# One-go logits, an early first list and waiting remainders in a convolution with mixture of experts

## The chip, the cores and the metric

The kernel runs on one core of one Trainium2 chip. Its time is the device time of one execution in microseconds (us), as a median over runs. PE is the matrix engine (TensorE), DVE the vector engine, ACT the scalar engine, POOL the general engine that issues the scatters here, and SP the engine that issues nearly all other transfers (DMAs). Each engine runs its own instructions strictly in program order and waits, where it must, for the others.

## The reference

A causal convolution over each sequence, whose seven weights per token and head are a softmax, is followed by a mixture of experts in which each token goes to one group of experts and to one expert in it:

```python
w = np.exp(weight_gen - max); w = w / (sum + 1e-09)          # (8, 2880, 8 heads, 7)
out = einsum('bshk,bskhg->bshg', w, x_unfolded)              # 192 = 8 heads x 24
g_idx = argmax(x @ w_group)                                  # 4 groups, weight g_w from their softmax
e_idx = argmax(xg @ w_expert[g])                             # 4 experts of the group, weight e_w
h = np.maximum(xg[mask_e] @ w1[g, e], 0.0)                   # 192 -> 1024
out[tok_idx] = (g_w * e_w)[:, None] * (h @ w2[g, e])         # 1024 -> 192
```

There are 8 × 2880 = 23040 tokens of 192 numbers and 16 experts in all, everything in 32-bit floats.

## The kernel before

The tokens are cut into 15 groups of 1536 (128 partitions × 12 rows), a group into two chunks of 6 rows per partition. For one group after the other `front()` yields the work of the convolution and of the routing in small steps, and a planner, which keeps a clock of its own for each engine (`clk`, `run`), writes the steps into one program order per engine. `Until(t)` holds a step back until the planner's DVE clock is at t, `NEXT` until one more unit is written, `Chunk(o, n)` until n chunks of the group are done. `move(qs, q, most)` takes up to `most` steps of a side task. After the planner nothing is reordered: what stands behind a waiting instruction on its engine waits too.

**Convolution.** `conv(g, o)` makes seven products per chunk on DVE (L280, tile `pr`, three buffers). In the first ten chunks (`TURNED = 10`, groups 0 to 4) PE adds each product and turns it over in the same step, by nine matmuls with the identity (L319, into three pieces of PSUM named `ph`, `py` and `tpx`). Such a set of nine is called a unit here. After a chunk's seventh unit ACT copies the three pieces out (L325, tiles `hl` and `xlo`). In later chunks DVE adds (L298) instead. `softmax(g)` (L255 to L268) makes a group's seven weights, on DVE with one exp on ACT.

**Routing.** `route(g, o)` turns the sums of a group back into rows (L390 on PE, called a back here, and L400 on ACT, into `xrow`), makes the logits (L365), turns them (L417), copies them to `ls` (L420), finds group and expert by `first_max` on DVE, counts tokens per expert with matmuls, and gets from that the position of each row (`posi`, L483). Twelve scatters on POOL (L513) then put the rows of the group into `rows` in memory, sorted by expert. At the end of each round of groups (`ROUNDS`; the first, `FIRST = 2`, is groups 0 and 1) `table` writes the work list `tab` (L590, L595).

**Visits.** A visit takes one block of rows of one expert through both matrices. The first round has ten plain visits of 128 rows, 0 to 9: SP reads the list (L745, L754), loads the rows (L746, tile `xb`), w1 (L757, two loads into `wa`) and w2 (L766, `wc`); PE turns the rows (L833) and does the two products, called gemm1 (L865) and gemm2 (L892). The later rounds have main visits of 256 rows (L841 turns their rows), with w1 split in two parts of lower precision: ACT casts (L779, L782), DVE subtracts (L797). The last 64 rows of w1 have their remainders ready in memory, as `w1lo`. The units of conversion and routing of later groups lie between the matmuls of the visits.

**Remainders.** `halves()` makes `w1lo` once, in eight pieces of two experts: loads on SP (L603, tile `raw`), cast on ACT (L612), subtract on DVE (L614), two stores on SP (L616). Before, it has two buffers, and a piece's loads are asked one piece ahead. The pieces are spread over the convolution of the first groups: one step in every fourth product, and the rest when the first main round comes up.

**Fillers.** `warm()` (L214) writes matmuls of no use into a free corner of PSUM where the planner thinks that PE would wait before the visits begin.

`blocks()` starts a round's visits: it asks the loads of the first visits in the order w1, w2, rows, one visit after the other.

Of the kernel before, what the change touches and what calls it, by code (L numbers as in the profile page):

```python
# [8 lines left out]
F32 = mybir.dt.float32  # L9
# [23 lines left out]
def conv_moe_kernel(ctx: ExitStack, tc: tile.TileContext, x, wgen, w_group, w_expert, w1, w2, out):  # L33
# [156 lines left out]
    state = {"slots": False, "open": False, "unit": 0, "starve": False, "ph": 0, "junk": None}  # L190
# [80 lines left out]
    sums, evac, spread = [], [], []  # L271
# [79 lines left out]
    def route(g, o):  # L351
# [17 lines left out]
        xTs = []  # L369
        txT = 0.0  # L370
        for s2 in range(0, SG, 2):
            n, i = s2 // SC, s2 % SC // 2
            if o.chunks <= n:
                yield Chunk(o, n + 1)
            row = xrow[n][:, s2 % SC:s2 % SC + 2, :]
            turned = n in o.turned
            if turned:
                txT = max(txT, evac[-1])
            elif i == 0:
                rem = rt.tile([P, SC, HP], F32, name="rem")  # L380
                nc.scalar.copy(out=rem, in_=xrow[n][:, :, P:D])
                txT = run("act", 0.4, clk["dve"])
                yield NEXT
            warm(txT)
            ttp = run("pe", 0.35, txT)
            tp = ps_t.tile([P, 3, P], F32, name="tp")
            if turned:
                xT = o.turned[n][i]
                for c in range(3):
                    nc.tensor.transpose(out=tp[:, c, :], in_=xT[:, c, :], identity=ident)  # L390
            else:
# [3 lines left out]
            if len(xTs) == 2:  # L395
                run("pe", 0.5, txT)
                logits(s2 - 4, xTs)
                xTs = []
            if turned:
                nc.scalar.copy(out=row[:, :, 0:D], in_=tp.rearrange("p c q -> p (c q)").rearrange("p (s d) -> p s d", s=2))  # L400
                run("act", 0.48, ttp)
            else:
# [3 lines left out]
            xTs.append((xT, turned))  # L406
            yield NEXT
        run("pe", 0.5, txT)
        logits(SG - 4, xTs)
# [3 lines left out]
        yield NEXT  # L413
# [6 lines left out]
        nc.scalar.copy(out=ls, in_=lps.rearrange("p q (j l) -> p (q j) l", l=LW)[:, :, 0:NL])  # L420
        for c, row in enumerate(xrow):
            nc.vector.tensor_copy(out=row.bitcast(I32)[:, :, D + 1:D + 2], in_=ii[:, s0 + c * SC:s0 + (c + 1) * SC].unsqueeze(2))
        yield 0.3
        yield Until(run("act", 0.4, clk["pe"]) + LATE[1])
# [35 lines left out]
        yield Until(tt + LATE[0])  # L460
# [25 lines left out]
        if g < MAIN:  # L486
            yield from finish_all(spread)
        if 0 < g < MAIN or g + 1 == ENDS[-1]:
            for c in rest:
                if g >= MAIN:  # L490
                    yield c
            if g + 1 in ENDS:
                yield from table(round_of(g))
            return
# [104 lines left out]
    def halves():  # L599
        def fetch(e):  # L600
            raw = new_raw[0]()
            for h in range(2):
                nc.sync.dma_start(out=raw[h * HP:(h + 1) * HP, :], in_=w1v[e + h, P:D, :])  # L603
            return raw

        hi = new_raw[2]()[:, 0:F].bitcast(F32R)
        nxt = fetch(0)
        for e in range(0, NE, 2):
            raw = nxt
            if e + 2 < NE:  # L610
                nxt = fetch(e + 2)
            nc.scalar.copy(out=hi, in_=raw)  # L612
            yield Until(run("act", 0.95))
            nc.vector.tensor_tensor(out=raw.bitcast(F32R), in0=raw, in1=hi.bitcast(F32), op=ALU.subtract)  # L614
            for h in range(2):
                nc.sync.dma_start(out=w1lo[e + h], in_=raw[h * HP:(h + 1) * HP, :])  # L616
            yield 1.13

# [15 lines left out]
    def front():  # L634
# [4 lines left out]
        slow = [[halves(), None]]  # L639
        yield from softmax(0)  # L640
        for g in range(ENDS[-1]):
            o = grp[g]
            routes.append([route(g, o), None])
            for n, c in enumerate(conv(g, o)):
# [6 lines left out]
                if n % 4 == 2:  # L651
                    for q in list(slow):
                        yield from move(slow, q, 1)
                for q in side[:1]:
                    yield from move(side, q, 3)
# [4 lines left out]
            if g + 1 == MAIN:  # L660
                yield from finish_all(slow)
# [67 lines left out]
    def load(n, part):  # L729
# [12 lines left out]
        if part == 0:  # L742
# [9 lines left out]
            return  # L752
        if o.ev is None:
            o.ev = nc.sync.value_load(tab[q:q + 1, 1:2], min_val=0, max_val=NE - 1)  # L754
# [179 lines left out]
    def blocks(n0, n1, paced):  # L934
# [59 lines left out]
        for n in range(n0, min(n0 + 2, n1)):  # L994
# [109 lines left out]
```

## Time and profile before

| | us |
|---|---|
| time before, median of 3 runs (1261.15 to 1261.85) | 1261.33 |
| time of the profiled execution | 1262.81 |
| its span | 1261.1 |
| opening, to visit 0's first matmul | 143.76 |
| ten plain visits, to the first turning of main rows | 102.12 |
| passage, to the first main gemm1 | 13.66 |
| main visits and tail | 1001.56 |

PE is busy for 1200.4 us of the span (95%), DVE for 921.7 (73%), ACT for 662.9 (53%) and POOL for 421.4 (33%). The granted clock of PE is 0.984 of the full speed on average. An engine's busy time includes the fillers. The span is what the profiler records between the first and the last instruction, and the time of the execution is a little longer.

### The profile page before, as it was taken

The page shows a single profiled execution, that of the slowest core. Times are in us where ns is not written, and L with a number is a line of the kernel's source. Part 1 is how long each engine was busy: PE and PEld are TensorE (multiplying, and loading weights), DVE is VectorE, ACT ScalarE, POOL GpSimd, SP SyncE. Part 2 cuts the span into 40 slices and gives each one's busy share as a digit, 9 for nine tenths or more (in the row PEclk, how much of TensorE's full clock was granted, in tenths as well). Part 3 has the DMA queues.
Part 4 walks back from the last instruction along what each step waited for, and adds up shares of the span by engine and source line. Part 5 has one row for each costly group of instructions (what it writes and reads, how often), then busy time and mean ns, then how long its engine had stood idle before and what let it go on. Part 6 is the DMA issues. An engine that isn't in the chain of part 4 may idle for free.

```text
span 1261.1 us, 26794 instructions
## 1 busy us (share of the span) xinstructions
PE 1200.4 (95%) x9559; PEld 1170.2 (93%) x9559; DVE 921.7 (73%) x1582; ACT 662.9 (53%) x1242; POOL 421.4 (33%) x412
## 2 busy tenths in 40 slices
PE   5998599899999999999999999999999999999995
PEld 5987599889999999999999999999999999999995
DVE  8974568788989999898899889961227677777500
ACT  1222133355555556555655565555556677767532
POOL 3043144143435243443524343453153311221111
PEclk9999799989999999999999999999999999999998
DMA  7447677988788879796979797778677877777792
GB/s 211 137 124 214 178 234 208 296 243 268 222 280 237 272 219 283 213 303 195 288 209 302 220 281 205 227 219 240 188 221 238 257 233 222 222 229 211 209 265 54
DMA packets 181678, 286.10 MB, mean 227 GB/s; under 512 B 16084, under 2 KB 141775, under 8 KB 181280
## 3 DMA queue, kind: packets, MB, share of 16 engines
q1 hardware_dynamic: 162304, 245.09, 66.6%
q0 software_dynamic: 19232, 39.22, 9.5%
q8 instruction: 77, 1.26, 0.4%
q14 instruction: 65, 0.53, 0.1%
HBM read 240.89 MB, written 44.33 MB: 226 GB/s over the span
## 4 chain that ended last, share of the span: by engine, by line
PE 62%; issue 19%; POOL 4%; DMA 3%; SPq 1%; POOLq 1%; DVE 1%; ACT 1%; ACTq 0%
PE py L892 27%; PE ph L865 26%; POOL out L909 3%; PE pl L365 2%; DMA raw<-in_moe_w 2%; PE tpx L841 1%; PE tpx L842 1%; PE tp L393 1%; PE ph L319 1%; PE py L319 1%; PE tpx L319 1%; DMA raw<-w1lo 1%; DMA rows<-xrow,posi 1%; PE tp L394 1%; POOLq L566 1%
## 5 line engine op out<-in xcount | busy, mean ns | idle before, releaser
L865 PE MATMUL ph<-xh,wa 128*128 128x256 f32 x2064 | 459.1, 299 | 0.0
L892 PE MATMUL py<-wc,hh 128*128 128x192 f32 x2240 | 417.6, 327 | 7.4 <-ACT xb L901 7.3
L909 POOL DMA_INDIRECT out<-xb x190 | 206.0, 1084 | 626.2 <-ACT xb L901 412.2
L892 PEld LDWEIGHTS py<-wc,hh 128*128 128x128 f32 x2240 | 359.6, 190 | 7.8 <-ACT xb L901 7.8
L865 PE MATMUL ph<-xlo,wa 128*128 128x256 f32 x1376 | 358.8, 282 | 0.0
L865 PEld LDWEIGHTS ph<-xh,wa 128*128 128x128 f32 x2064 | 350.1, 190 | 7.4 <-issue 5.9
L871 ACT ACTIVATE hh<-ph 128x512 f32<-128x512 f32 (+1 forms) x316 | 173.4, 549 | 314.8 <-PE ph L865 314.8
L280 DVE TENSOR_TENSOR pr<-xin,wt 128x1152 f32<-128x1152 f32 x190 | 253.8, 1352 | 18.2 <-PE tpx L319 18.1
L865 PEld LDWEIGHTS ph<-xlo,wa 128*128 128x128 f32 x1376 | 261.9, 190 | 0.0
L513 POOL DMA_INDIRECT rows<-xrow,posi x180 | 196.3, 1091 | 181.1 <-DVE posi L483 56.5
L797 DVE TENSOR_TENSOR wa<-raw,wa 128x1024 fp32r<-128x1024 f32 x86 | 105.0, 1221 | 83.6 <-ACT wa L779 81.8
L298 DVE TENSOR_TENSOR xrow<-xrow,pr 128x1152 f32<-128x1152 f32 x120 | 162.4, 1353 | 0.6
L894 PE MATMUL py<-wc,hh 128*128 128x384 f32 x400 | 122.6, 362 | 0.8 <-DVE xb L907 0.8
L797 DVE SCALAR_TENSOR_TENSOR hl<-ph,hh 128x512 fp32r<-128x512 f32 x100 | 69.1, 691 | 67.8 <-ACT hh L876 67.5
L895 PE MATMUL py<-wc,hl 128*128 128x192 f32 x400 | 100.6, 251 | 0.0
L779 ACT CAST wa<-raw 128x1024 fp32r<-128x1024 f32 x86 | 90.3, 1050 | 8.9 <-DMA raw<-in_moe_w 8.9
L782 ACT CAST wa<-raw 128x1024 fp32r<-128x1024 f32 x86 | 89.5, 1040 | 0.3 <-DMA raw<-w1lo 0.3
L901 ACT ACTIVATE xb<-py,xb 128x192 f32<-128x192 f32 x190 | 71.7, 421 | 27.5 <-PE py L892 21.9
L865 PE MATMUL ph<-xd,wa 96*128 96x128 f32 x576 | 77.3, 277 | 0.5 <-ACT xd L835 0.5
L894 PEld LDWEIGHTS py<-wc,hh 128*128 128x128 f32 x400 | 76.0, 190 | 1.2 <-DVE xb L907 1.2
L895 PEld LDWEIGHTS py<-wc,hl 128*128 128x128 f32 x400 | 77.1, 193 | 0.0
L797 DVE TENSOR_TENSOR xlo<-tpx,xh 128x512 fp32r<-128x512 f32 x86 | 59.2, 688 | 23.2 <-ACT xh L846 23.0
(165 smaller groups left out, 1326.4 us busy)
## 6 DMA issues: line engine op xcount, KB each, us to landing
wc<-in_moe_w SPq DMA_DIRECT2D x79, 768.0 KB, 7.6
raw<-in_moe_w SPq DMA_DIRECT2D x86, 512.0 KB, 4.2
raw<-in_moe_w SPq DMA_DIRECT2D x102, 256.0 KB, 4.3
xin<-in_x SPq DMA_DIRECT2D x26, 864.0 KB, 8.2
raw<-w1lo SPq DMA_DIRECT2D x86, 256.0 KB, 5.2
raw<-in_moe_w SPq DMA_DIRECT2D x25, 768.0 KB, 4.9
xb<-rows SPq DMA_DIRECT2D x86, 194.0 KB, 4.2
wa<-in_moe_w SPq DMA_DIRECT2D x36, 384.0 KB, 4.1
```

The source lines that it names most:

```text
L280: nc.vector.tensor_tensor(out=dst, in0=o.xin[:, c0 + k:c0 + k + SC, :].rearrange("p s (h g) -> p s h g", g=HG), in1=w4[:, c0:c0 + SC, :, k ...
L298: nc.vector.tensor_tensor(out=acc, in0=acc, in1=prs[k - 2], op=ALU.add)
L513: written_once(nc.gpsimd.indirect_dma_start(out=rows[:, :], out_offset=bass.IndirectOffsetOnAxis(ap=idx, axis=0), in_=src, in_offset=None, ...
L779: nc.scalar.copy(out=o.wa[:, 0, :], in_=o.raw[0])
L782: nc.scalar.copy(out=o.wa[:, 2, :], in_=o.raw[1])
L797: f(*a, **k)
L865: nc.tensor.matmul(ph[:, v, :], lhsT=w[:, f0:f0 + P], rhs=rhs, start=i == 0, stop=i == len(terms) - 1)
L871: nc.scalar.activation(out=hh, in_=ph, func=AF.Relu)
L892: nc.tensor.matmul(b.py[t][:, 0:D], lhsT=hh[:, v, c], rhs=wc[0][:, f, :], start=f == 0, stop=f == NFT - 1)
L894: nc.tensor.matmul(b.py[t], lhsT=hh[:, v, c], rhs=wc[f // 4][:, f % 4].rearrange("p l d -> p (l d)"), start=f == 0, stop=False)
L895: nc.tensor.matmul(b.py[t][:, 0:D], lhsT=hl[:, v, c], rhs=wc[f // 4][:, f % 4, 0, :], start=False, stop=f == NFT - 1)
L909: ins = nc.gpsimd.indirect_dma_start(out=out[:, :], out_offset=bass.IndirectOffsetOnAxis(ap=b.x.bitcast(I32)[:, t, D + 1:D + 2], axis=0), ...
```

## The change

All edits are in the planner and in the order of steps; the arithmetic stays.

- `route`: for groups with turned chunks the first chunk's three backs are written while the second chunk is convolved; after the second chunk come all 48 logits matmuls at once, one back, the turn of the logits, the copy to `ls`, and then the second chunk's other two backs. Other groups go the old way, in `forward()`.
- In groups 0 and 1 the planner's wait for `ls` and for the counts is 0.3 instead of `LATE`.
- `state["urgent"]` is set while group 2 (`FIRST`) is convolved and the first list isn't made; then the next group's softmax and the remainders stand still.
- `halves()` starts in group 1 and asks four pieces at once, into four buffers; subtracts come from group 2 on, after the first list; what is left is written before the first main weights.
- The scatters that are still to come are finished in one go before a list of an early round, and in the last groups' routing only every third is a step.
- `blocks()` asks the weights of the first three visits, then their three row loads.

```diff
-    sums, evac, spread = [], [], []
+    sums, evac, spread, slow = [], [], [], []
...
+        def back(n, i):
+            warm(evac[-1])
+            ttp = run("pe", 0.35, evac[-1])
+            tp = ps_t.tile([P, 3, P], F32, name="tp")
+            for c in range(3):
+                nc.tensor.transpose(out=tp[:, c, :], in_=o.turned[n][i][:, c, :], identity=ident)
+            nc.scalar.copy(out=xrow[n][:, 2 * i:2 * i + 2, 0:D], in_=tp.rearrange("p c q -> p (c q)").rearrange("p (s d) -> p s d", s=2))
+            run("act", 0.48, ttp)
...
+        turned = 2 * g < TURNED
+        if turned:
+            for i in range(NP):
+                back(0, i)
+                yield NEXT
+            yield Chunk(o, 2)
+            warm(evac[-1])
+            run("pe", 1.2, evac[-1])
+            flat = [(t, True) for n in range(2) for t in o.turned[n]]
+            for q in range(SG // 4):
+                logits(4 * q, flat[2 * q:2 * q + 2])
+        else:
+            yield from forward()
         lts = rt.tile([P, 3, P], F32, name="xT", bufs=2)
         nc.scalar.copy(out=lts, in_=lt)
         tlt = run("act", 0.48, clk["pe"])
-        yield NEXT
+        if turned:
+            back(1, 0)
+        else:
+            yield NEXT
...
+        tls = run("act", 0.4, clk["pe"])
+        if turned:
+            for i in range(1, NP):
+                back(1, i)
...
-        yield Until(run("act", 0.4, clk["pe"]) + LATE[1])
+        yield Until(tls + (0.3 if g < FIRST else LATE[1]))
...
-        yield Until(tt + LATE[0])
+        yield Until(tt + (0.3 if g < FIRST else LATE[0]))
...
         if g < MAIN:
-            yield from finish_all(spread)
+            while spread:
+                for c in spread.pop(0)[0]:
+                    pass
         if 0 < g < MAIN or g + 1 == ENDS[-1]:
-            for c in rest:
-                if g >= MAIN:
+            for i, c in enumerate(rest):
+                if g >= MAIN and i % 3 == 2:
                     yield c
             if g + 1 in ENDS:
                 yield from table(round_of(g))
+            state["urgent"] = False
             return
...
     def halves():
         def fetch(e):
-            raw = new_raw[0]()
+            raw = new_raw[e // 2 % 2]()
             for h in range(2):
                 nc.sync.dma_start(out=raw[h * HP:(h + 1) * HP, :], in_=w1v[e + h, P:D, :])
-            return raw
+            return raw, clk["dve"]
 
         hi = new_raw[2]()[:, 0:F].bitcast(F32R)
-        nxt = fetch(0)
+        got = [fetch(2 * e) for e in range(4)]
+        yield Until(clk["dve"] + 10.0)
         for e in range(0, NE, 2):
-            raw = nxt
-            if e + 2 < NE:
-                nxt = fetch(e + 2)
+            raw, t = got.pop(0)
+            yield Until(t + 18.0)
             nc.scalar.copy(out=hi, in_=raw)
...
             yield 1.13
+            if e and e + 6 < NE:
+                got.append(fetch(e + 6))
...
+            state["urgent"] = g == FIRST
             for n, c in enumerate(conv(g, o)):
...
-                if n % 4 == 2:
+                if g == FIRST - 1 and n == 4:
+                    slow.append([halves(), None])
+                    yield from move(slow, slow[0], 1)
+                if g >= FIRST and n % 2 == 0 and not state["urgent"]:
                     for q in list(slow):
-                        yield from move(slow, q, 1)
-                for q in side[:1]:
-                    yield from move(side, q, 3)
+                        yield from move(slow, q, 2)
+                if not state["urgent"]:
+                    for q in side[:1]:
+                        yield from move(side, q, 3)
...
-            if g + 1 == MAIN:
-                yield from finish_all(slow)
...
+        if not plain(n):
+            while slow:
+                assert step() is not False
...
-            ask(n, 0)
         if n0 + 2 < n1 and plain(n0 + 2):
             ask_w(n0 + 2)
-        ask_x(n0 + 2)
+            ask(n0 + 2, 3)
+        for n in range(n0, min(n0 + 3, n1)):
+            ask(n, 0)
+        if n0 + 2 < n1 and not plain(n0 + 2) and (whole(n0 + 2) or whole(n0 + 1)):
+            ask(n0 + 2, 3)
```

SP, behind visit 1's weights, before: the third visit's row load (`xb_160`), its w2, the last remainder's loads (L603) and four stores (L616), and group 4's weights (L238).

```order
L746 DMA xb_160<-rows 128x194
L766 ISA
L766 DMA wc<-in_moe_w 128x8x192
L603 DMA raw_170<-in_moe_w 64x1024 x2
L616 DMA w1lo<-raw_171 64x1024 x2
L616 DMA w1lo<-raw_170 64x1024 x2
L238 DMA wt<-in_weight_gen 128x672
```

The same place on SP in the changed program, where the row load is L770, the remainders' loads L623 and their stores L636:

```order
L770 DMA xb_160<-rows 128x194
L232 DMA xin<-in_x 128x1728
L636 DMA w1lo<-raw_171 64x1024 x2
L636 DMA w1lo<-raw_173 64x1024 x2
L623 DMA raw_171<-in_moe_w 64x1024 x2
L636 DMA w1lo<-raw_170 64x1024 x2
L623 DMA raw_173<-in_moe_w 64x1024 x2
L636 DMA w1lo<-raw_172 64x1024 x2
L623 DMA raw_170<-in_moe_w 64x1024 x2
L238 DMA wt<-in_weight_gen 128x672
```

The loads of the first four pieces (171, 173, 170, 172) have moved far ahead of this place, ahead of the first read of a list; the loads of three later pieces stand here instead, each behind the store that frees its buffer.

DVE, from the end of the first list (`done`) to the first maximum of group 2's routing, before:

```order
L561 SCALAR_TENSOR_TENSOR done<-tk,done 128x16
L280 TENSOR_TENSOR pr<-xin,wt 128x1152 x2
L422 COPY xrow<-ii 128x6 x2
L614 TENSOR_TENSOR raw_171<-raw_171,raw_174 128x1024
L614 TENSOR_TENSOR raw_170<-raw_170,raw_174 128x1024
L280 TENSOR_TENSOR pr<-xin,wt 128x1152
L333 TENSOR_REDUCE mxg<-ls 128x12
```

The same engine in the changed program, from the end of the first list (L581) on; L634 is the remainders' subtract, L255 to L268 is the softmax of group 3:

```order
L581 SCALAR_TENSOR_TENSOR done<-tk,done 128x16
L280 TENSOR_TENSOR pr<-xin,wt 128x1152
L255 TENSOR_REDUCE m<-wt 128x96
L257 TENSOR_TENSOR wt<-wt,m 128x672
L280 TENSOR_TENSOR pr<-xin,wt 128x1152 x2
L262 TENSOR_REDUCE z<-wt 128x96
L264 TENSOR_SCALAR z<-z 128x96
L266 RECIPROCAL z<-z 128x96
L634 TENSOR_TENSOR raw_171<-raw_171,raw_174 128x1024
L268 TENSOR_TENSOR wt<-wt,z 128x672
L280 TENSOR_TENSOR pr<-xin,wt 128x1152 x3
L634 TENSOR_TENSOR raw_173<-raw_173,raw_174 128x1024
```

Two products of chunk 5 were left when the list was done, ten are left now, and the subtracts have moved from the far side of the list to this one.

PE, the end of chunk 5's routing, before: backs (L390) and logits (L365) in turn, the logits' turn (L417), 60 fillers and chunk 6's first unit (L319).

```order
L390 MATMUL tp<-ident,xlo 128x128 x3
L365 MATMUL pl<-hl,wr 32x128 x8
L390 MATMUL tp<-ident,xlo 128x128 x3
L365 MATMUL pl<-xlo,wr 32x128 x8
L214 MATMUL py_1273<-ident 128x128 x2
L417 MATMUL pl<-ident,xT 128x128 x3
L214 MATMUL py_1273<-ident 128x128 x60
L319 MATMUL ph_1715<-ident,pr 128x128 x3
```

The same place on PE in the changed program, where a back is L374, the logits' turn L430, and L860 and L892 are visit 0's turn and gemm1:

```order
L214 MATMUL py_1398<-ident 128x128 x11
L365 MATMUL pl<-hl,wr 32x128 x16
L365 MATMUL pl<-xlo,wr 32x128 x8
L374 MATMUL tp<-ident,hl 128x128 x3
L430 MATMUL pl<-ident,xT 128x128 x3
L374 MATMUL tp<-ident,xlo 128x128 x6
L860 MATMUL tp<-ident,xb_158 96x128 x2
L892 MATMUL ph_1584<-xd_167,wa 128x128 x4
```

Visit 0's matmuls now stand directly behind chunk 5's routing, and chunk 6's first unit behind them.

SP, behind the weights of a main visit shortly before the first main gemm1, before: an input load (L232) stands between w1 of one visit and the rows of another.

```order
L762 DMA raw_172<-w1lo 64x1024
L232 DMA xin<-in_x 128x1728
L745 TENSOR_LOAD tab_1943
L745 ISA x2
L746 ISA
L746 DMA xb_160<-rows 128x388
```

The same place in the changed program:

```order
L789 DMA raw_172<-w1lo 64x1024
L769 TENSOR_LOAD tab_1908
L769 ISA x2
L770 ISA
L770 DMA xb_160<-rows 128x388
```

The input load has moved behind the w1 loads of three more main visits.

## Rows read from the trace of the kernel before

**Rows 1.** Stretches: length, engines' busy us (count), PEclk, DMA share, GB/s.
```profile
0.00:143.76 143.76, 107.81 (x993) 98.87 (x994) 104.66 (x200) 31.54 (x60) 35.08 (x50) 0.94 0.62 175
143.76:245.88 102.12, 100.69 (x883) 95.99 (x882) 82.54 (x167) 37.26 (x93) 36.63 (x32) 1.00 0.76 233
245.88:259.54 13.66, 6.33 (x35) 6.14 (x33) 5.64 (x7) 3.97 (x8) 0.97 (x1) 0.67 0.91 239
259.54:1261.10 1001.56, 985.61 (x7654) 969.22 (x7652) 728.83 (x1211) 590.13 (x1081) 348.74 (x329) 0.99 0.79 233
```

**Rows 2.** Waits in 0 to 262 us: total us, times, longest us.
```profile
PE ph L319 <- DVE pr L280: 30.9, 5, 15.0
DVE raw L614 <- ACT raw L612: 27.5, 2, 16.4
```

**Rows 3.** The chain in 105 to 146 us: start us, length us, what.
```profile
110.25 6.74 DMA rows<-xrow,posi
...
117.14 0.36 SPq L746
...
124.89 1.34 SPq L603
126.27 10.51 DMA raw<-in_moe_w
...
139.10 1.36 DVE pr L280
...
140.51 0.90 PE ph L319 x3
```

**Rows 4.** Three short or typical stretches, columns as in rows 1.
```profile
130.00:140.00 10.00, 0.00 (x0) 0.00 (x0) 2.04 (x2) 1.04 (x1) 0.00 (x0) 0.50 0.68 176
250.00:255.00 5.00, 0.00 (x0) 0.00 (x0) 0.74 (x1) 1.82 (x4) 0.00 (x0) 0.55 1.00 240
300.00:600.00 300.00, 300.00 (x2338) 293.31 (x2338) 271.65 (x456) 174.19 (x324) 121.21 (x106) 1.00 0.81 247
```

**Rows 5.** DVE in order of time: start, length, instruction, count, [idle before <-releaser].
```profile
79.18 1.36 DVE L280 TENSOR_TENSOR pr<-xin,wt 128x1152 f32<-128x1152 f32 x1 [6.56 <-PE tpx L319]
...
94.76 0.17 DVE L483 SCALAR_TENSOR_TENSOR posi<-pos 128x12 int32<-128x12 f32 x1
...
105.89 0.15 DVE L595 TENSOR_SCALAR tab<-ri 128x1 int32<-128x1 f32 x1
...
106.47 2.62 DVE L280 TENSOR_TENSOR pr<-xin,wt 128x1152 f32<-128x1152 f32 x2
```

**Rows 6.** DVE groups in 13.29 to 109.1 us: count, busy us, mean ns.
```profile
L280 DVE TENSOR_TENSOR pr<-xin,wt 128x1152 f32<-128x1152 f32 x42 | 55.0, 1352 | 6.9 <-PE tpx L319 6.9
L614 DVE TENSOR_TENSOR raw<-raw,raw 128x1024 fp32r<-128x1024 f32 x6 | 7.3, 1220 | 0.0
...
L255 DVE TENSOR_REDUCE m<-wt 128x96 f32<-128x672 f32 x3 | 2.5, 848 | 0.0
```

**Rows 7.** PE at chunk 5's end and visit 9's, as rows 5.
```profile
113.23 1.42 PE L214 MATMUL py<-ident 128*128 128x128 f32 x11 [0.29 <-ACT xlo L325]
...
115.55 0.55 PE L390 MATMUL tp<-ident,xlo 128*128 128x128 f32 x3 [0.57 <-ACT xrow L400]
...
117.14 0.65 PE L365 MATMUL pl<-xlo,wr 128*32 128x128 f32 x16
...
118.77 6.71 PE L214 MATMUL py<-ident 128*128 128x128 f32 x60
...
255.36 1.65 PE L892 MATMUL py<-wc,hh 128*128 128x192 f32 x4 [7.33 <-ACT xb L901]
```

**Rows 8.** POOL, first scatter of group 1, columns as in rows 5.
```profile
95.71 1.33 POOL L513 DMA_INDIRECT rows<-xrow,posi  x1 [11.38 <-issue]
```

**Rows 9.** The chain in 222 to 262 us, columns as in rows 3.
```profile
244.38 8.70 DMA raw<-in_moe_w
```

**Rows 10.** The page's DMA issues: count, KB each, median us to landing.
```profile
xb<-rows SPq DMA_DIRECT2D x86, 194.0 KB, 4.2
```

More of the change, by code (lines that the diff above doesn't have):

```diff
@@ L189, in conv_moe_kernel @@
     grp = {}
-    state = {"slots": False, "open": False, "unit": 0, "starve": False, "ph": 0, "junk": None}
+    state = {"slots": False, "open": False, "unit": 0, "starve": False, "ph": 0, "junk": None, "urgent": False}
     def ph_tile(k, shape):
@@ L367, in logits, with forward @@
                         start=u == 0, stop=u == 1, tile_position=(0, j * LW))
[L369 to L382, printed above, removed]
-                yield NEXT
-            warm(txT)
-            ttp = run("pe", 0.35, txT)
-            tp = ps_t.tile([P, 3, P], F32, name="tp")
[L387 to L391, printed above, removed]
+        def back(n, i):
+            warm(evac[-1])
+            ttp = run("pe", 0.35, evac[-1])
+            tp = ps_t.tile([P, 3, P], F32, name="tp")
+            for c in range(3):
+                nc.tensor.transpose(out=tp[:, c, :], in_=o.turned[n][i][:, c, :], identity=ident)
+            nc.scalar.copy(out=xrow[n][:, 2 * i:2 * i + 2, 0:D], in_=tp.rearrange("p c q -> p (c q)").rearrange("p (s d) -> p s d", s=2))
+            run("act", 0.48, ttp)
+        def forward():
+            xTs = []
+            for s2 in range(0, SG, 2):
+                n, i = s2 // SC, s2 % SC // 2
+                if o.chunks <= n:
+                    yield Chunk(o, n + 1)
+                row = xrow[n][:, s2 % SC:s2 % SC + 2, :]
+                if i == 0:
+                    rem = rt.tile([P, SC, HP], F32, name="rem")
+                    nc.scalar.copy(out=rem, in_=xrow[n][:, :, P:D])
+                    txT = run("act", 0.4, clk["dve"])
+                    yield NEXT
+                ttp = run("pe", 0.35, txT)
+                tp = ps_t.tile([P, 3, P], F32, name="tp")
                 for u in range(2):
@@ L394, in route @@
                 nc.tensor.transpose(out=tp[:, 2, :], in_=rem[:, s2 % SC:s2 % SC + 2, :].rearrange("p s d -> p (s d)"), identity=ident)
[L395 to L402, printed above, removed]
+                if len(xTs) == 2:
+                    run("pe", 0.5, txT)
+                    logits(s2 - 4, xTs)
+                    xTs = []
                 xT = rt.tile([P, 3, P], F32, name="xT", bufs=2)
@@ L405, in route @@
                 txT = run("act", 0.48, ttp)
[L406 to L409, printed above, removed]
+                xTs.append((xT, False))
+                yield NEXT
+            run("pe", 0.5, txT)
+            logits(SG - 4, xTs)
+        turned = 2 * g < TURNED
+        if turned:
+            for i in range(NP):
+                back(0, i)
+                yield NEXT
+            yield Chunk(o, 2)
[6 more added lines that the diff above has]
+            yield from forward()
         lts = rt.tile([P, 3, P], F32, name="xT", bufs=2)
@@ L412, in route @@
         tlt = run("act", 0.48, clk["pe"])
-        yield NEXT
+        if turned:
+            back(1, 0)
+        else:
+            yield NEXT
         warm(tlt)
@@ L638, in front @@
         load_group(1)
-        slow = [[halves(), None]]
         yield from softmax(0)
```

## The prediction

> **What bounds the kernel now.** I read the span by stretches first. The reader is to see four stages [rows 1]: 143.76 us before visit 0, the ten plain visits (102.12 us, with PE busy for 100.69), a passage of 13.66 us to the first main visit, and the main visits with the tail (1001.56 us). A middle stretch of the last stage has PE busy for all of its 300 us [rows 4], and the whole stage for 985.61 of 1001.56. So only the first three stages have time to give, and the last one shifts as a whole if PE stays its bound.
>
> In the opening PE is busy for 107.81 of 143.76 us, but 395 of the matmuls that the order has there are fillers (L214). DVE is busy for 104.66, and it sets the pace until chunk 5's last products, which end at 106.47 + 2.62 = 109.1 [rows 1, 5]. Then the waits: of 30.9 us that PE waits for a product, 15.0 are one wait, and DVE waits twice for a cast, the longer time 16.4 us [rows 2]. The chain shows that knot [rows 3]. SP stands behind the row load of visit 0, which waits until group 1's last scatter, issued at 110.25, has landed at 117.0; weights and row loads of three visits follow; only at 124.89 does SP issue the load of the last w1 remainder, which takes 10.51 us; cast, subtract, product and unit follow, the unit at 140.51. The product is in program order behind two subtracts on DVE, and visit 0 on PE is behind that product's unit. Visit 0 itself could have run about 20 us earlier. While PE stood, its granted clock was 0.50 [rows 4].
>
> **Part 1: remainders out of the way.** DVE's order shows no L614 ahead of the first list instead of six, three before chunk 5's last product, and none between it and visit 0 that waits for a transfer asked for behind the row load: the first four pieces are now loaded before group 3's inputs, on SP ahead of the first list's loads. In the order PE goes from chunk 5's last routing matmuls straight to visit 0; the chunk-6 unit that stood between is behind it.
> To chunk 5's last product DVE does the same 42 products in both programs, the same three softmaxes and two routings, and three subtracts less: 3 × 1.22 = 3.7 us [rows 6]. From the old 109.1 that gives 105.4.
>
> **Part 2: logits in one go.** This adds waits on DVE. Before, a routing's logits came piece by piece between units; now 48 matmuls stand behind the second chunk's copies. From the end of a chunk's last product to ls: a unit of nine transposes at the filler's 6.71/60 = 0.11, so 1.0; copies 0.29 + 1.42 (fillers cover them); logits at most 3 × 0.65 = 1.9; copy, transposes and copy about 1.5. That is 6.1 us, less the next chunk's first two products (2.6): 3.5 us of waiting in each of two routings, 7.0 in all, and about 1.4 for positions behind fillers and for a cast. The old program waited 6.9 there, 6.56 of it once [rows 5, 6]. So +1.5 (bounds 0 and +5): the last product ends at about 107.0. The list comes far earlier. Ahead of group 1's positions the order has two products less (32 for 34, 2 × 55.0/42 = 2.6 us), five subtracts less (6.1) and one softmax less (six operations of 0.2 to 0.9 us, the first of them 0.85 [rows 6], an estimated 4.3), against 1.5 of waits: 94.76 − 11.5 = 83.3. Six products and a subtract stood between positions and table before, none now, so the table stands at about 86 instead of 105.89.
> From there to visit 0, step by step: unit 1.0, copies 1.7, logits 1.9, and three backs with their copies 2.4 (a back waits 0.57 for its copy [rows 7], a pitch near 1.1). Sum 7.0: **visit 0 at 114.0 instead of 143.76, a gain of 29.8.** The cross-check by what goes: from 118.77 to 143.76 25.0 us of fillers, idle PE and one unit; the rest are 2.1 on DVE and 2.7 in the shorter end of the chunk.
> Are the rows there? Scatters start 0.95 us after positions and go at (110.25 − 95.71)/11 = 1.32 [rows 5, 8]: the last at about 98.8, landed 6.74 later at 105.5, and a row load of 4.2 us [rows 10] ends at 109.7. That leaves 4.3 us.
>
> **Part 3: weights before rows, for three visits.** SP asks all three visits' weights (3 × 1.5 MB) as soon as the table stands, then the row loads. In the old order two of the three stood behind the row load that waited to 117. At the 233 GB/s that the visits moved [rows 1] 4.6 MB are 20 us, from 86 to 106. At that rate they are done as the row load goes, and cost nothing: scatters and PE's own work cover them. If that cover is gone, it is rival A.
>
> **Part 4: the plain visits.** Of 70 units 28 instead of 27 lie behind visit 0: +1.0. The logits in one go of two groups meet PE without other work: 2 × 1.2 = 2.4 (0 to 5). Four subtracts move in here: 4 × 1.22 = 4.9 on DVE, busy for 82.54 of 102.12 us, so I take nothing on PE. Their four loads and all eight stores move in too, some 4 MB more beside 23.8 MB (233 GB/s × 102 us); DMA share goes from 0.76 to about 0.88. SP also has stores that wait for subtracts ahead of group 4's weights; 1.0 for that (0 to 5). Sum +4.4: main's first matmuls follow at about 220.5, plus the passage.
>
> **Part 5: the passage.** Before, PE stood 7.33 us [rows 7] behind a weight load of 8.70 us [rows 9], with DMA at 0.91, and the work at its end ran at a clock near 0.5 [rows 4]. In the order of SP one input load, 128 × 1728 × 4 B = 0.88 MB, leaves this place, to behind the w1 of three more visits. At this stretch's 239 GB/s [rows 1] it is 3.7 us of DMA time; I take 3.2 of them off the wait, and 1.2 for a shorter time at half clock: 13.66 − 4.4 = 9.2. The bounds are 5 (no wait: 13.66 − 7.33 and the half clock with it) and 16 (the same wait with 2 us more for fuller DMA).
>
> **Part 6: the rest.** The planner's waits of 0.3, the spread finish and the late scatters touch lists that are far ahead of main. Lists of group 5 on come about one visit later in the order, against a lead of many visits. I take zero (−3 to +4). 103 fillers less (428 to 325) are no gain of their own; they covered waits.
>
> **Sum.** −29.8 + 4.4 − 4.4 + 0 = −29.8. The profiled run took 1262.81 with a span of 1261.1, so 1233.0 for such a run; it lies 1.5 above the median of 1261.33, against which the forecast is **1231.5 us**.
>
> **Rivals.**
> *A, late rows or weights (13%).* The 4.6 MB asked first share the DMA engines with group 1's scatters. For it: a w1 piece took 10.51 us in a crowd, a weight load 8.70 [rows 3, 9], and the margin is 4.3. If the scatters land at 118 instead of 105.5, the row load ends at about 122.5 and visit 0 starts at 123: 1231.5 + 9 = 1240 (1236 to 1243). Against it: the scatters are small and in the old trace ran beside other loads.
> The Trainium skill, "DMA: Bandwidth & Descriptors", section "Issuing engines are not separate DMA queues", says that transfers started by different engines run on the same 16 DMA engines and interleave. By that rule alone the scatters would pay for the early weights, which speaks against this order and gives A's time; the trace of before has no such moment, its scatters ran beside halves alone.
> *B, the visits are no longer PE's (15%).* The remainders' 4 MB and 4.9 us of DVE come on top of DMA at 0.76 and DVE at 82.54/102.12 = 0.81. If DVE with its waits becomes the bound, 82.5 + 4.9 + some 25 us of softmax waits or late inputs as at the passage make the stage 112 to 117 us: 1231.5 + 6 to 15 = 1237 to 1247. For it: the passage shows what DMA near 0.9 does. Against: PE waited under 2 us in this whole stage.
> *C, the clock (3%).* Fewer fillers could let the granted clock fall to half in the opening. The rows show a fall after PE stood 15.0 and 7.3 us, none after waits of 0.57. New waits here are of that short kind. A chunk's seven units at half clock cost 7 us more: about 1239.
> The Trainium skill, "TensorE: Matmul & The Clock Gate", section "Why this matters for your kernels", advises against idle gaps between bursts of matmuls, since the clock drops; this case's trace agrees, with 0.50 in the 15.0-us gap. A drop in the opening would lead to C's time.
> *D, slower (3%).* The old knot returns for the remaining four pieces: a subtract stands in DVE's program order ahead of a product, its load on SP behind a store or a row load that waits. Each such turn would cost what the last one did, 139.10 − 124.89 = 14.2 us; it is slower from the third on, and four make 57 less 29.8: 1288.
> *E, no gain at the end (4%).* Main waits for lists, not for PE, and the shift is lost: about 1261. Against it: no PE idle in 300 us [rows 4].
>
> **How the numbers follow.** Forecast 62%, A 13, B 15, C 3, D 3, E 4. The forecast's own range by the bounds is 1223 to 1237; the range that holds 8 in 10 goes over A and B: 1223 to 1247. A measurement tells about 0.2% (2.5 us). Faster 0.93 (forecast, A, B, C), same 0.04 (E), slower 0.03 (D).
>
> **What would show it.** Group 1's positions near 83; the row load on SP near 106; visit 0 near 114, with no PE gap over 3 us and no clock near 0.5 before it; no long wait of the subtract for its cast; the stage of plain visits at about 106.5; the wait at the passage near 4 instead of 7.33; main's stage at about 1001.6. A row load behind 112 means A, a stage over 110 means B, long subtract waits in the visits D, a longer main stage E. Wrong above all would be the forecast if visit 0 waited for something other than PE's own order.

## The result, and the profile after

The changed kernel takes 1242.73 us (median of 4 runs, 1241.98 to 1243.15) beside 1261.24 for the kernel before: 18.5 us less, a ratio of 0.985 (95% interval 0.984 to 0.987). The forecast was 1231.5 with a range of 1223 to 1247. So the sign and the range hold, but 11.3 of the 29.8 us of gain are missing, and the time lies outside the forecast's own range of 1223 to 1237.

The stages of the profiled run, cut at the same instructions as [rows 1] (visit 0's turn, the first turn of main rows, the first main gemm1); columns are the stretch, its length, the engines' busy us and counts, PEclk, DMA share and GB/s:

```profile
0.00:115.36 115.36, 93.59 (x882) 86.69 (x882) 99.91 (x194) 27.62 (x55) 39.54 (x50) 1.00 0.54 161
115.36:226.83 111.47, 104.56 (x892) 100.41 (x893) 81.78 (x166) 40.70 (x98) 37.14 (x32) 0.97 0.88 267
226.83:238.75 11.92, 6.33 (x35) 6.13 (x33) 5.25 (x7) 3.86 (x8) 0.97 (x1) 0.73 0.95 257
238.75:1241.50 1002.75, 985.54 (x7654) 969.64 (x7652) 735.71 (x1216) 589.91 (x1081) 350.38 (x329) 0.99 0.77 234
```

| stage, us | before | forecast | after | after − forecast |
|---|---|---|---|---|
| opening | 143.76 | 114.0 | 115.36 | +1.4 |
| ten plain visits | 102.12 | 106.5 | 111.47 | +5.0 |
| passage | 13.66 | 9.2 | 11.92 | +2.7 |
| main and tail | 1001.56 | 1001.6 | 1002.75 | +1.2 |
| span | 1261.1 | 1231.3 | 1241.5 | +10.2 |

The opening went nearly as worked out. Of what answers to [rows 5] and [rows 7], DVE's and PE's timelines of the changed kernel show group 1's positions at 83.32 (forecast 83.3, before 94.76), the table at 85.64 (86; 105.89), chunk 5's last products ending at 107.65 (107.0; 109.1), the predicted wait for `ls`, and visit 0:

```profile
73.61 0.20 DVE L333 TENSOR_REDUCE mxg<-ls 128x12 f32<-128x48 f32 x1 [3.40 <-ACT ls L433]
...
83.32 0.17 DVE L500 SCALAR_TENSOR_TENSOR posi<-pos 128x12 int32<-128x12 f32 x1
...
85.64 0.15 DVE L615 TENSOR_SCALAR tab<-ri 128x1 int32<-128x1 f32 x1
...
105.03 2.62 DVE L280 TENSOR_TENSOR pr<-xin,wt 128x1152 f32<-128x1152 f32 x2
```

```profile
115.36 0.43 PE L860 MATMUL tp<-ident,xb 128*96 128x128 f32 x2 [0.57 <-ACT xrow L375]
116.24 1.99 PE L892 MATMUL ph<-xd,wa 96*128 96x128 f32 x8 [0.46 <-ACT xd L862]
```

The new loss lies in the plain visits, where PE now stands for 111.47 − 104.56 = 6.9 us (before 1.4). Its chain in 118 to 150 us (start, length, what) answers to [rows 3]; it is the old knot at a new place:

```profile
123.32 0.51 SPq L636
...
124.57 0.86 SPq L623
...
125.53 0.99 SPq L623
...
126.56 5.97 DMA wt<-in_weight_gen
...
132.56 0.86 DVE m L255
...
133.44 0.87 DVE wt L257
...
135.01 0.36 ACT hh L898
135.37 0.25 ACT xd L862
135.63 0.33 ACT xb L928
...
136.00 0.92 PE py L919 x4
```

The reader is to see five engines in a row. SP issues stores (L636) and refills (L623) of the remainders, and only behind them the weights of group 4 (`wt`), at 126.56. DVE's softmax waits for these. ACT's exp (L258) waits for DVE, and in ACT's program order the plain visit's three copies stand behind that exp; they go only at 135.01 to 135.63. PE waits 4.19 us for the last of them:

```profile
134.34 0.76 ACT L258 ACTIVATE wt<-wt 128x672 f32<-128x672 f32 x1 [5.83 <-DVE wt L257]
...
136.00 0.92 PE L919 MATMUL py<-wc,hh 128*128 128x192 f32 x4 [4.19 <-ACT xb L928]
```

SP's own timeline shows why it was late:

```profile
111.61 3.87 SPq L636 DMA_DIRECT2D w1lo<-raw  x4
118.45 1.14 SPq L623 DMA_DIRECT2D raw<-in_moe_w  x2
119.69 1.18 SPq L636 DMA_DIRECT2D w1lo<-raw  x2
120.92 2.25 SPq L623 DMA_DIRECT2D raw<-in_moe_w  x2
123.22 1.25 SPq L636 DMA_DIRECT2D w1lo<-raw  x2
124.57 1.94 SPq L623 DMA_DIRECT2D raw<-in_moe_w  x2
126.56 0.58 SPq L238 DMA_DIRECT2D wt<-in_weight_gen  x1
```

Each refill overwrites a buffer whose store must have landed first; SP stands at the first one for 3 us. The later ones find their stores landed. From 118.45 to 126.56 SP does nothing but issue: 5.3 us for the six refill loads and 2.4 us for the four stores between them, an issue taking 0.5 to 1.4 us (why so long stays open). The stall has a second price, a lower granted clock (the column behind the five engines' busy times):

```profile
136.00:138.00 2.00, 2.00 (x11) 1.98 (x12) 1.93 (x9) 0.22 (x1) 0.97 (x1) 0.71 1.04 174
138.00:140.00 2.00, 2.00 (x11) 2.00 (x10) 1.97 (x4) 0.00 (x0) 1.39 (x1) 0.50 1.08 282
```

### The profile page after: what moved, and what is told of

The parts are those of the page before. It is cut to its first block, busy times and chain, and to the rows that moved or that the text cites. A ratio compares the mean times of both kernels' runs of the same rounds, so it can differ in the third digit from the quotient of the medians.

```text
span 1241.5 us, 26600 instructions
## 1 busy us (share of the span) xinstructions
PE 1190.0 (96%) x9456; PEld 1162.9 (94%) x9456; DVE 922.6 (74%) x1582; ACT 662.1 (53%) x1242; POOL 428.0 (34%) x412
## 4 chain that ended last, share of the span: by engine, by line
PE 67%; issue 20%; DVE 4%; POOL 4%; DMA 3%; ACT 1%; SPq 0%; POOLq 0%; DVEq 0%; ACTq 0%
PE py L919 27%; PE ph L892 27%; POOL out L936 3%; PE pl L365 2%; PE ph L319 1%; PE py L214 1%; DVE pr L280 1%; PE py L319 1%; PE tpx L319 1%; PE tpx L868 1%; PE tpx L869 1%; PE tp L393 1%; DMA raw<-in_moe_w 1%; PE tp L374 1%; DMA wc<-in_moe_w 1%
## 5 line engine op out<-in xcount | busy, mean ns | idle before, releaser
L892 PE MATMUL ph<-xh,wa 128*128 128x256 f32 x2064 | 459.7, 299 | 0.0
L919 PEld LDWEIGHTS py<-wc,hh 128*128 128x128 f32 x2240 | 359.9, 191 | 10.2 <-ACT xb L928 10.2
L892 PE MATMUL ph<-xlo,wa 128*128 128x256 f32 x1376 | 359.4, 283 | 0.0
L892 PEld LDWEIGHTS ph<-xh,wa 128*128 128x128 f32 x2064 | 351.0, 191 | 7.4 <-issue 5.9
L892 PEld LDWEIGHTS ph<-xlo,wa 128*128 128x128 f32 x1376 | 262.5, 191 | 0.0
L533 POOL DMA_INDIRECT rows<-xrow,posi x180 | 201.9, 1122 | 133.2 <-DVE posi L500 57.2
L892 PE MATMUL ph<-xd,wa 96*128 96x128 f32 x576 | 78.8, 281 | 0.5 <-ACT xd L862 0.5
L892 PEld LDWEIGHTS ph<-xd,wa 96*128 96x128 f32 x576 | 75.1, 198 | 0.8 <-ACT xd L862 0.7
```

What stands on the lines that cost most here:

```text
L533: written_once(nc.gpsimd.indirect_dma_start(out=rows[:, :], out_offset=bass.IndirectOffsetOnAxis(ap=idx, axis=0), in_=src, in_offset=None, ...
L892: nc.tensor.matmul(ph[:, v, :], lhsT=w[:, f0:f0 + P], rhs=rhs, start=i == 0, stop=i == len(terms) - 1)
L919: nc.tensor.matmul(b.py[t][:, 0:D], lhsT=hh[:, v, c], rhs=wc[0][:, f, :], start=f == 0, stop=f == NFT - 1)
```

## The experiments

Theory Q (queue): the missing time went to the order in which SP issues loads, where one that waits, or is only issued earlier, holds back another that somebody needs. Theory C (crowd): the remainders' loads and stores, moved into the plain visits, slow all transfers there, whatever their order. Each ratio below is against the kernel before in the same session. The first four runs and the last fell on two chips where the kernel before itself took 1390 and 1376 us, with standstills of some 10 us now and then that the profile can't place; these five are compared only with the kernel before beside them, and the changed kernel itself was not run there.

**Remainders from group 3 on only.**

```diff
-                if g >= FIRST and n % 2 == 0 and not state["urgent"]:
+                if (g > FIRST and n > 2 or g > FIRST + 1) and n % 2 == 0:
```

> The changed kernel, with the remainders' subtracts, stores and refills only from group 3's third product on, so that on SP they stand behind the load of group 4's weights. Theory Q (the queue): the visits lost about 7 us to SP's order, 4.2 of PE standing and the rest at half clock behind it; then this run is at 1236 to 1238, the stage of plain visits at 104 to 106 us, and DVE's 8-us wait for the weights is gone. Theory C (the crowd): the 4 MB of remainders slow all transfers wherever they stand; then 1242 to 1244 and a stage near 111.

1383.97 against 1389.96 (ratio 0.995, 0.992 to 0.998). **No remainders at all** (the main visits read rows of w1 in the place of `w1lo`):

> The changed kernel without the remainders: no loads, casts, subtracts or stores of them; the main visits read rows of w1 in their place, the same number of bytes. It bounds all that the remainders cost. Theory Q: about the time of the run that asks the weights first, 1235 to 1238, with the passage still near 12 us. Theory C: clearly below that run, 1229 to 1233, visits at 103 to 104 and the passage under 10.

1366.09 against 1389.96 (0.984, 0.979 to 0.989). **The old asking order** of the first visits' loads:

> The changed kernel with the first visits' loads asked in the old order, each visit's rows ahead of the next visit's weights. If early weights are worth something: visits 1 and 2 wait for weights that are asked only at 108 us and land after 116 to 122, +2 to +6, 1245 to 1249. If PE's own order hides it: 1242 to 1244. If the early weights hold back the scatters (rival A of the prediction): faster, 1238 to 1241.

1370.86 (0.986, 0.980 to 0.991). **The kernel before with the remainders' part alone** (four pieces up front, subtracts after the list):

> The kernel before with only the remainders' part of the change: four pieces asked up front, subtracts after the first list, no softmax or remainder moved to behind it otherwise. If the knot of the last subtract was most of the loss: visit 0 at 118 to 121 instead of 143.76, and 1238 to 1244 in all, as good as the whole change, since the weights of group 4 stand ahead of the stores on SP here. If the one-go logits and the early list carry much of the gain: 1247 to 1253.

1399.98 (1.007, 1.004 to 1.010). Nothing in these four tells Q from C: their stages hold standstills like the following, on the chain of the third run in 64 to 86 us, long before the places in dispute. They are inconclusive, and the last two were run again elsewhere.

```profile
69.28 12.41 another core or an unknown queue
```

**The changed kernel again**, as the mark for three others on one chip:

> The changed kernel once more, as the mark for the runs beside it on the same chip: 18.5 us under the kernel before, 1242 to 1244 where that takes 1261. On a chip whose transfers are slower the gain may differ; then the runs beside it are read against this one alone.

1242.11 against 1262.93 (0.983, 0.981 to 0.985; 1238.13 to 1243.42). Its profiled run, at 1238.60 us the second shortest of five, has the same chain 1.9 us earlier: the weights go out at 124.64 and PE waits 1.42 us at that place instead of 4.19. The clock stays at 1.00 behind it, and the plain visits take 107.48 us. So about 4 us of the stage hang on this one wait.

**Refills behind group 4's weights.**

```diff
-        got = [fetch(2 * e) for e in range(4)]
+        got, due = [fetch(2 * e) for e in range(4)], []
...
             if e and e + 6 < NE:
-                got.append(fetch(e + 6))
+                due.append(e + 6)
+            while due and (state["refill"] or not got):
+                got.append(fetch(due.pop(0)))
...
                     load_group(g + 1, (n // 8,))
+                    state["refill"] = g > FIRST
```

> The changed kernel with the remainders' refills (the loads of pieces 5 to 8, each of which waits on SP for a store to land) asked only behind group 4's weights, all but one; stores and subtracts of the first four pieces stay. Theory Q (SP's queue holds the weights back): the weights go out at about 119 instead of 126.6 us, DVE's wait of 8 us for them goes or shrinks under 2, PE's 4.2-us wait in the visits goes with the half clock behind it: 5 to 7 us under the changed kernel, 1236 to 1238. Theory C (crowded transfers, wherever they stand in the queue): within 2 us of the changed kernel.

1238.20 (0.982, 0.980 to 0.983), 3.9 us under the mark by the medians, but the two ranges overlap (this one is 1237.66 to 1242.69). Its stretches of the plain visits and of the passage, and the weights on SP:

```profile
115.21:220.45 105.24, 102.22 (x902) 98.29 (x903) 80.34 (x166) 40.84 (x98) 38.87 (x32) 1.00 0.90 277
220.45:233.65 13.20, 6.33 (x35) 6.14 (x33) 6.09 (x9) 3.97 (x8) 0.97 (x1) 0.76 1.01 251
```

```profile
120.03 0.59 SPq L238 DMA_DIRECT2D wt<-in_weight_gen  x1
```

The weights go out 6.5 us earlier than in the first result and 4.6 earlier than in the mark, DVE still waits 3.46 us for them, but PE has no wait over 1 us in the visits. Their stage is 105.24, under the forecast's 106.5, at a DMA share of 0.90. The same transfers in another order: that speaks for Q, for the visits. The time hardly shows it, since the gain comes back at the passage, where PE now waits 6.87 us: visits and passage together take 118.4 us, and 118.5 in the mark's profiled run (107.48 and 11.03).

**Fillers ahead of visit 0**: five matmuls behind each of the last two backs, and four that were meant to stand ahead of the first gemm1.

> The changed kernel with 5 fillers behind each of chunk 5's last two backs and 4 ahead of visit 0's first product, where PE waited 0.57, 0.57 and 0.46 us and then ran for about 3.5 us at a clock of 0.50. If these short waits brought the clock down, it stays at 1.00 here and the visits' stage is 1.5 to 2 us shorter: 1240.5 to 1241.5. If something else did it (the small matmuls before, the change of kind), the dip stays and the time is that of the changed kernel.

1240.26 (0.982, 0.981 to 0.983). Only the ten behind the backs stand where they were meant to. The other four ended up far ahead in PE's order and ran 34 us before visit 0's turn, so the 0.46-us wait ahead of gemm1 stays:

```profile
L1051 PE MATMUL py<-ident x4: 272/272/273, 81.5 to 81.8; 128*128 128x128 f32 x4
```

Visit 0's first eight matmuls take 1.16 us instead of 1.99, and the clock stays at 1.00:

```profile
116.21 1.16 PE L899 MATMUL ph<-xd,wa 96*128 96x128 f32 x8 [0.46 <-ACT xd L869]
```

The median is 1.85 us under the mark, about as expected, but the intervals overlap, and the profiled run's visits are not shorter: they take 112.15 us, because the weights go out at 126.61 and PE waits 5.22 us at the old place. Nor is the dip behind visit 0's turn there in every profiled run: three of kernels without these fillers show it (0.50 in 118 to 119 us), two don't, and neither of the two with fillers does. That fillers prevent it is possible, not shown.

**The remainders' part alone, again:**

> The kernel before with only the remainders' part of the change, once more beside the changed kernel on one chip. If the knot of the last subtract was nearly all: within 3 us of the changed kernel. If the early list and the one-go logits carry a large part: 5 to 12 us above it, with visit 0 at 119 to 124.

1251.82 (0.992, 0.990 to 0.994): 11.1 of 20.8 us. Its opening, visits and passage:

```profile
0.00:120.65 120.65, 99.67 (x934) 91.03 (x935) 97.33 (x187) 25.53 (x53) 35.37 (x50) 1.00 0.48 144
120.65:235.02 114.37, 101.22 (x866) 96.28 (x865) 88.64 (x178) 43.06 (x100) 36.00 (x32) 0.96 0.90 275
235.02:249.54 14.52, 6.33 (x34) 6.13 (x33) 5.49 (x8) 3.97 (x8) 0.97 (x1) 0.69 0.98 235
```

Undoing the old knot gives 23.1 of the opening's 28.4 us; one-go logits, the early list and the early weights give the other 5.3. But 12 us go again in the visits: PE waits 8.65 us there for ACT, where the exp that waits for group 4's weights stands ahead of visit 0's first copy. These weights were issued at 118.79, behind those of visits 1 and 2, and took 7.89 us to land where they took 5.97 in the changed kernel. So a crowd may account for about 2 us of the wait; the rest is order again. The time is 9.7 us above the mark, as the second expectation has it.

**The old asking order, again**, on a chip with the transfers of the first result:

> The changed kernel with the first visits' loads asked in the old order, each visit's rows ahead of the next visit's weights, on a chip with the transfers of the first result. If the early weights of visits 1 and 2 matter: they go out at 107 to 110 us, land after 116, and visits 1 and 2 and group 4's weights behind them come late: 3 to 6 us above the changed kernel. If PE's own order hides them: within 1.5 us of it.

1248.50 against 1262.47 (0.989, 0.987 to 0.991): a gain of 14.0 us where the changed kernel has 18.5 and 20.8 in its two sessions, so 4 to 7 us worse. The visits take 117.45 us. The chain in 95 to 140:

```profile
100.24 3.50 DMA rows<-xrow,posi
...
106.03 7.93 DMA wc<-in_moe_w
113.98 9.28 DMA w1lo<-raw
...
131.40 5.89 DMA wt<-in_weight_gen
```

The late weights of visits 1 and 2 fall together with the stores, at a DMA share of 1.08 in 111 to 118 us (0.86 in the changed kernel); a store takes 9.28 us to land, SP stands at its refill until 122.7, and group 4's weights go out at 131.40. PE then waits 10.76 us. So crowd and queue seem to work together, as far as one run shows it: the crowd makes a store slow, and the queue hands the delay to a load that has nothing to do with it.

**Visit 11's w1 with visit 10's.** At the passage the changed kernel's SP shows this, w1 of visits 10, 12 and 11 in that order:

```profile
209.56 1.48 SPq L786 DMA_DIRECT2D raw<-in_moe_w  x1
...
221.99 0.34 SPq L786 DMA_DIRECT2D raw<-in_moe_w  x1
...
224.84 0.35 SPq L786 DMA_DIRECT2D raw<-in_moe_w  x1
```

Visit 12 uses visit 10's buffer, which DVE leaves at 221.97. Visit 11's own buffer has been free since the remainders, but its load stands behind. PE pays for it:

```profile
234.57 1.65 PE L919 MATMUL py<-wc,hh 128*128 128x192 f32 x4 [5.59 <-ACT xb L928]
```

The kernel before has the same order of the three loads:

```profile
230.76 0.34 SPq L759 DMA_DIRECT2D raw<-in_moe_w  x1
...
241.52 0.33 SPq L759 DMA_DIRECT2D raw<-in_moe_w  x1
...
244.38 0.34 SPq L759 DMA_DIRECT2D raw<-in_moe_w  x1
```

```diff
-                if end and n + 3 < n1 and (plain(n + 3) or plain(n + 1)):
+                if end and n + 3 < n1 and (plain(n + 3) or plain(n + 2)):
                     ask_w(n + 3)
+                    if not plain(n + 3):
+                        ask_w(n + 4)
```

> The changed kernel with visit 11's w1 asked together with visit 10's. In the trace SP asks visit 12's w1 ahead of visit 11's; its buffer is visit 10's, so SP stands until 221.99 us, and visit 11's w1, whose own buffer has long been free, goes out at 224.84; ACT stands at its cast with plain visit 9's last copy behind it, and PE waits 5.59 us. Theory Q (SP's order): the wait at the passage goes to under 1.5 us, no half clock behind it, the passage is 5 to 7 us instead of 11.9, and the time 5 to 7 under the changed kernel: 1236 to 1238 where that takes 1242. Theory C (crowded transfers, 0.95 of the DMA engines busy there): w1 comes earlier, but w2 or w1lo of visit 10 come later for it; a passage of 10 to 13 and 1241 to 1244.

1235.52 against 1262.47 (0.979, 0.977 to 0.981): a gain of 27.0 us where the changed kernel has 18.5 and 20.8, so 6 to 8 us better. The passage, and the two loads:

```profile
224.39:228.44 4.05, 4.05 (x35) 4.05 (x33) 3.64 (x6) 3.26 (x8) 0.97 (x1) 1.00 1.07 230
```

```profile
207.13 0.35 SPq L786 DMA_DIRECT2D raw<-in_moe_w  x1
...
210.64 0.35 SPq L786 DMA_DIRECT2D raw<-in_moe_w  x1
```

PE is busy for all of it, at full clock, though the DMA engines are at 1.07. That decides for Q at this place.

**All three orders together:**

> The changed kernel with refills behind group 4's weights, fillers ahead of visit 0, and visit 11's w1 asked with visit 10's. If the three losses are apart from each other: 4 + 1.5 + 6 = 11 us under the changed kernel, 1230 to 1232 where that takes 1242, with the visits near 104 and the passage near 6. If what the visits gain is given back at the passage, as the first of the three alone showed by 1 to 2 us: 1234 to 1237.

1229.26 against 1262.47 (0.975, 0.973 to 0.977; 1228.19 to 1234.02): a gain of 33.2 us, 12 to 15 more than the changed kernel's. The first expectation holds, the gains add up. Beside the run with only visit 11's w1 moved, in the same session, the other two edits are worth 6.3 us, 4.1 of them in the visits, and the two intervals of the ratio don't touch. That is the gain which the passage had hidden:

```profile
0.00:115.67 115.67, 94.80 (x895) 88.14 (x895) 100.05 (x194) 27.64 (x55) 38.58 (x50) 1.00 0.55 164
115.67:220.92 105.25, 102.22 (x902) 98.29 (x903) 81.08 (x166) 41.24 (x99) 38.91 (x32) 1.00 0.92 278
220.92:224.97 4.05, 4.05 (x35) 4.05 (x33) 4.02 (x7) 3.26 (x8) 0.97 (x1) 1.00 1.04 307
224.97:1227.70 1002.73, 985.02 (x7654) 968.66 (x7652) 737.26 (x1217) 589.86 (x1082) 351.19 (x329) 0.99 0.79 236
```

Seven profiled runs that differ in when SP comes to issue group 4's weights, side by side (us):

| run | weights go out | DVE starts on them | PE's longest wait in the visits | visits | DMA share |
|---|---|---|---|---|---|
| all three orders | 119.67 | 125.68 | 0.6 | 105.25 | 0.92 |
| refills behind weights | 120.03 | 126.23 | 0.6 | 105.24 | 0.90 |
| changed kernel again | 124.64 | 129.51 | 1.42 | 107.48 | 0.91 |
| visit 11's w1 early | 124.93 | 130.12 | 2.04 | 109.34 | 0.91 |
| changed kernel | 126.56 | 132.56 | 4.19 | 111.47 | 0.88 |
| fillers ahead of visit 0 | 126.61 | 131.91 | 5.22 | 112.15 | 0.85 |
| old asking order | 131.40 | 137.32 | 10.76 | 117.45 | 0.88 |

From issue to use the weights take 4.9 to 6.2 us in all seven. PE's wait and the stage follow the moment of issue, and not the DMA share.

**The kernel before with visit 11's w1 early**, nothing else:

> The kernel before with nothing changed but visit 11's w1 asked together with visit 10's. If the wait at the passage is this order of two loads alone, in the kernel before as in the changed one: passage 4 to 5 us instead of 13.66, 8.5 to 9.5 us less, 1252 to 1254 where the kernel before takes 1262. If the fuller DMA and the input load that stood there (the prediction's account) were part of it: the passage is 7 to 10, 1256 to 1259.

1366.58 against 1375.96 on a chip of the slower kind (0.993, 0.989 to 0.996): 9.4 us less, between 6 and 15. Its passage is 6.08 us long, between the two expectations, with PE busy for 5.97 of them at a clock of 0.72, just behind a wait of 2.75 us for the rows. The wait for visit 11's w1 is gone there too, and the size fits the first expectation, but on such a chip it doesn't exclude the second.

## Why the prediction was right, and where its sum was not

**The range** held in part by luck. The forecast's own range was 1223 to 1237; 1242.73 lies in the stated one because that was widened for rivals A and B. By the prediction's own sign, a stage of plain visits over 110, it was B, but neither late rows (A) nor DVE or a crowded DMA as the bound (B) is what happened, as follows.

**Parts 1 and 2 (the opening)** held step by step: 28.4 us of the forecast 29.8. The waits for `ls` are 3.3 and 3.4 us where 3.5 was worked out, the end of chunk 5 to visit 0 takes 7.7 where 7.0 was. The remainders' part alone brings 23.1 of it.

**Part 3 and rival A.** The early weights do hold the rows back: with the old asking the last scatter lands 3.50 us after its issue and the row load goes at 103.86; with the early weights the row load goes at 106.92 and 106.99 in the same session, and at 107.92 in the first result. These 3 to 4 us lie inside the margin of 4.3, and visit 0 starts at 115.20 with the old asking, at 115.05 and 115.67 with the early weights. It cost nothing in the opening because PE's own order is what visit 0 waits for. The Trainium skill, "DMA: Bandwidth & Descriptors", section "Issuing engines are not separate DMA queues", says that transfers started by different engines run on the same 16 DMA engines and interleave. The trace agrees, with these row loads. One reading of the prediction was wrong: the trace of before does have such a moment. Its last scatter, issued at 110.25, followed the loads of visit 0's weights and took 6.74 us to land:

```profile
106.71 0.95 SPq L757 DMA_DIRECT2D wa<-in_moe_w  x2
```

The part was put at no gain. It is worth 4 to 7 us, all of it in the next stage.

**Part 4 (the plain visits) is the step that failed.** "SP also has stores that wait for subtracts ahead of group 4's weights; 1.0 for that (0 to 5)": the place was right, the price wrong. No store that waits for a subtract held SP up there, but the refills: 3 us in which the first stands for a store to land, and 5.3 us in which SP issues the six loads. Behind `wt` stand DVE's softmax, ACT's exp and, in ACT's order, three copies that PE needs. The term measured 6.2 us (111.47 less 105.24), 4.2 of standing and some 2 of half clock, part of it the dip behind visit 0's turn. The amount of data was too low as well: the stage moved 267 GB/s × 111.47 us = 29.8 MB, 6 more than before, not some 4. The rest of the part was right: without that wait the stage is 105.25 where 106.5 was forecast, so the extra unit, the backs and DVE's subtracts cost 3.1 of the 3.4 that were put down.

**Rival B** is what happened in its time (1237 to 1247) and in its place, late inputs in the visits. Its condition, a DMA share near 0.9 and DVE's load, was not the cause: the versions without the wait have shares of 0.90 and 0.92 and the same work on DVE.

**Rival C (the clock)** took a small part that I had excluded with "none after waits of 0.57": behind visit 0's turn, after waits of 0.57, 0.57 and 0.46 us in a row, the clock is 0.69 in 116 to 117 us, 0.50 in 117 to 119 and 0.61 in 119 to 120; this comes and goes between runs. After the 1.42-us wait of the second run the clock stayed at 1.00. The Trainium skill, "TensorE: Matmul & The Clock Gate", section "Why this matters for your kernels", advises against idle gaps between bursts of matmuls, since the clock drops. The trace agrees for the single gap, with 0.50 behind the 4.19-us wait; the dip behind the three short waits stands on the traces alone.

**Part 5 (the passage) had a wrong mechanism.** It took the wait for a crowded transfer and 3.2 us off it for the input load that moved away. The wait shrank from 7.33 to 5.59 only, and asking two loads in the other order takes it away entirely, at a DMA share of 1.04 to 1.07 where the passage had 0.91 before. The one line of [rows 9] gives the 8.70 us that the load took, but not why it was issued only at 244.38; SP's order in the trace of before shows that, with visit 12's load ahead of it. Issued 14 us earlier, the load lands in time. D did not come, since every subtract found its cast within 1.8 us; E did not, since main's stage stayed at 1002.75.

## What to carry to other kernels

A load behind a waiting load or store on the same issuing engine inherits that wait, and each issue ahead of it costs time too (0.5 to 1.4 us here): go through the issue order around each buffer that is reused, and ask for what has a free buffer and an early consumer first. When a knot is undone, look for the next in-order queue that the moved instructions enter; here the same pieces that had held PE from DVE's queue held it from SP's, one stage later. A stall's price is read from the stage in which nothing else waits, and includes what PE does at half clock behind it.

## What the runs showed of the hardware that was not expected

The granted clock fell to 0.50 behind a single wait of 4.19 us and behind one of 2.04 us, not behind one of 1.42, and it fell behind visit 0's turn in three of five profiled runs with the same instructions and the same waits there. On two of the four chips of the experiments all versions took about 10% longer, with standstills of up to 12.4 us of ACT and PE that the profile puts down to an unknown queue; what these wait for stays open.
